# Renumbering the inner columns of a two-matrix expert layer: long rows of w_out, stepped weights from w_in

## The chip, the core and the metric

The kernel runs on one core of a Trainium2 chip. A core has a matrix engine (PE, TensorE, which loads weights and then streams columns past them), three engines for element work (DVE is VectorE, ACT is ScalarE, POOL is GpSimd), a queue engine for transfers (SP), and 16 DMA engines between the DRAM and the on-chip memory of 128 partitions. PE writes into accumulators (PSUM), from which ACT and DVE copy. The metric is the device time of one execution in microseconds; the median of several runs is compared.

## The reference

Attention with sketched features, followed by an expert layer with a rational activation:

```python
x = attention(q, k, v, S1, S2)          # 4352 tokens x 128
h = x @ w_in                            # w_in 128 x 2048
P = a[0] + a[1] * h + a[2] * h**2 + a[3] * h**3
Q = 1.0 + abs(b[0]) * abs(h) + abs(b[1]) * h**2
out = (P / (Q + 1e-6)) @ w_out          # w_out 2048 x 128
```

q, k and v are 4 batches x 4 heads x 1088 positions x 32, in float32. The 2048 inner columns of `h` are only ever used one by one and then summed over by `w_out`, so any numbering of them gives the same result as long as the columns of `w_in` and the rows of `w_out` are numbered alike.

## The kernel before

The attention part makes `xT`, a 128 x 4352 float32 tile with the model dimension on the partitions, batch by batch. The expert part runs over 17 units: one of the first 256 tokens, 14 for seven blocks of 512 tokens (each block in two units, one for each half of the inner columns), and two of 256 tokens at the end. A unit always has 4096 columns of work per partition, made of inner blocks of 128 columns by its tokens: 16 blocks by 256 tokens or 8 blocks by 512.

In a unit, `hidden` (line 448) multiplies: the weights are a 128 x 128 block of `w_in`, the moving operand is a stretch of `xT`; the result, 128 inner columns on the partitions by the tokens, goes to one of two `h_ps` accumulators. Everything there is float32, and one such product runs as two passes, each with its own weight load. There are 48 products of 256 columns and 112 of 512. ACT copies each accumulator to bf16 (`hh`, `evac`, line 454); DVE and ACT make |h|, the denominator, its reciprocal by logarithm and exponential, and the terms r, s and g (lines 477 to 562). `gather` (line 581) multiplies these with `w_out` as weights, in bf16, and adds all up in one accumulator for each block of tokens; `store` (line 590 on) transposes and writes the result.

The order of all instructions is written out by hand in `ORDER`, a list of steps such as `lw:1` (fetch half 1 of `w_out`), `lx:0` (fetch half 0 of `w_in`), `wo:3` (make a scaled bf16 copy of half of `w_out`), `h2:5` (line 448 for part 2 of unit 5) or `e2:5` (its copy). Each engine runs its own instructions in that order and waits only for the data and the buffers that it needs. Nothing is rescheduled at run time.

The fetches all go through SP's queue. After the first batch's k, q and v its order is: half 1 of `w_out`, the rest of q, half 0 of `w_out`, half 1 of `w_in`, the second batch's k, half 0 of `w_in`, the second batch's q and v. `w_out` is 1 MB in all, as is `w_in`; each half is 512 KB. `w_out_sb_f` has a partition for each of the 128 rows of an inner block, and along it 16 blocks of 128 float32. It is read six times (lines 614, 616 and 618), to make the three bf16 copies that `gather` uses: each half plain, times a[1] and times a[2].

Before the change, inner column number `128 * fo + fi` is row `fi` of block `fo`. So a partition of `w_out_sb_f` is filled from 16 separate rows of 512 bytes each, and the weights of a product are 128 neighbouring columns of `w_in_sb`.

Of the kernel before, what the change touches and what calls it, by code (L numbers as in the profile page):

```python
# [59 lines left out]
SPLIT_A = (0, 9, 13, 16)  # L60
QUARTER = (16,)
LX = 2
TAIL = 2
WIDE_S = (3, 5)
WIDE_M = (5,)
# [4 lines left out]
def kernel(  # L70
# [13 lines left out]
    nc = tc.nc  # L84
# [5 lines left out]
    nf = d_ff // 128  # L90
# [48 lines left out]
    for i, s_in in enumerate((S1, S2)):  # L139
        t = consts.tile([128, D], FP, name=f"s_raw{i}")  # L140
# [4 lines left out]
                      in_=bass.AP(tensor=k.tensor, offset=k.offset, ap=[[S * D // 32, 128], [W, NM], [1, 4 * D]]))  # L145
    nc.scalar.dma_start(out=k0[:, 0:km].rearrange("p (m x) -> p m x", m=NM - 1)[:, :, 4 * D:],
                        in_=k0_src[:, 0:km].rearrange("p (m x) -> p m x", m=NM - 1)[:, :, 4 * D:])
# [11 lines left out]
    load_v(0)  # L159
    w_in_sb = big.tile([d_model, d_ff], FP, name="w_in_sb")  # L160
    w_out_sb_f = mid.tile([128, nf, d_model], FP, name="w_out_sb_f", tag="w", bufs=2)
    w_out_src = moe_w_out.rearrange("(fo fi) d -> fi fo d", fi=128)

    idle = consts.tile([128, 512], BF, name="idle")
    nc.vector.memset(idle, 0.0)
# [27 lines left out]
    for i in range(2):  # L193
        t = consts.tile([128, D], FP, name=f"sT{i}")
# [14 lines left out]
    for i in range(2):  # L209
        t = consts.tile([128, 2, R, R], FP, name=f"SAB{i}")  # L210
# [14 lines left out]
    def wide():  # L225
        return hps.tile([128, 1024], FP, name="h_ps")
# [205 lines left out]
    t1 = n_tok % TC  # L432
    last = TC // TAIL
    for t0, tl in [(0, t1)] * (t1 > 0) + [(t, TC) for t in range(t1, n_tok - TC, TC)] + [(t, last) for t in range(n_tok - TC, n_tok, last)]:
# [7 lines left out]
    def hidden(i, part):  # L442
        t0, tl, f0, per = units[i]
        assert ready.issuperset(range(t0, t0 + tl, 64))
        t = live[i]["h", part] = wide()
        for x in range(per // 4):
            f = f0 + part * (per // 4) + x
            nc.tensor.matmul(t[:, x * tl:(x + 1) * tl], lhsT=w_in_sb[:, f * 128:(f + 1) * 128],  # L448
                             rhs=xT[:, t0:t0 + tl], start=True, stop=True)

    def evac(i, part):
# [188 lines left out]

    def fetch_w(x):
        f = slice(x * (nf // 2), (x + 1) * (nf // 2))
        nc.sync.dma_start(out=w_out_sb_f[:, f], in_=w_out_src[:, f])

    def fetch_x(x):
        c = slice(x * (d_ff // 2), (x + 1) * (d_ff // 2))
# [4 lines left out]
    blocks = [lambda: QA, lambda: QB, lambda: QC, once(lambda: Spread(0, q0, cuts[3], cuts[4]))]  # L651
    blocks += [once(lambda b=b, c0=c0, c1=c1: Spread(b, fetched["lq", b], c0, c1)) for b in range(1, B) for c0, c1 in spans]
    does = {"e": evac, "h": hidden, "u": d_abs, "w": d_w, "y": d_y, "ln": a_ln, "ex": a_exp, "pa": a_p, "pd": d_p,
            "s": d_s, "m": d_hs, "v": d_v, "x": d_g, "G": gather}
    q_does = {"qt": "transposes", "qs": "sketches", "qc": "copies", "qf": "features", "qp": "products", "qd": "plus",
# [55 lines left out]
```

## Time and profile before

| | |
|---|---|
| median of 3 runs | 274.04 us (273.96 to 274.20) |
| the profiled execution | 274.08 us, of which its span is 272.3 us |
| granted PE clock | 0.999 |
| DMA | 30530 packets, 19.55 MB, mean 72 GB/s |
| line 448, passes of 512 columns | 224, together 103.7 us busy |
| line 448, passes of 256 columns | 96, together 22.5 us busy |
| line 448, weight loads | 320, 58.3 us busy |
| line 581, products with w_out | 460, in bf16 |

The span is the time from the first to the last instruction that the profile holds; a run's time also has what lies around it. PEld is the weight loading of PE, told apart from its matmuls because the two overlap. A matmul's recorded length holds more than its streaming time, so the pace of a series is read from starts, not from lengths. A share of busy time is a mean over the span. The first 20 us are those with the most transfer: the DMA engines move 166, 290 and 330 GB/s in the first three of 40 slices of the span.

### The profile page before, as it was taken

The page shows a single profiled execution, that of the slowest core. Times are in us where ns is not written, and L with a number is a line of the kernel's source. Part 1 is how long each engine was busy: PE and PEld are TensorE (multiplying, and loading weights), DVE is VectorE, ACT ScalarE, POOL GpSimd, SP SyncE. Part 2 cuts the span into 40 slices and gives each one's busy share as a digit, 9 for nine tenths or more (in the row PEclk, how much of TensorE's full clock was granted, in tenths as well). Part 3 has the DMA queues.
Part 4 walks back from the last instruction along what each step waited for, and adds up shares of the span by engine and source line. Part 5 has one row for each costly group of instructions (what it writes and reads, how often), then busy time and mean ns, then how long its engine had stood idle before and what let it go on. Part 6 is the DMA issues. An engine that isn't in the chain of part 4 may idle for free.

```text
span 272.3 us, 3730 instructions
## 1 busy us (share of the span) xinstructions
PE 258.4 (95%) x1398; PEld 146.2 (54%) x1398; DVE 256.0 (94%) x277; ACT 250.2 (92%) x224; POOL 2.9 (1%) x24
## 2 busy tenths in 40 slices
PE   7989999999999899999999999999999998999763
PEld 2778656963564354545454554434545356675552
DVE  2876999999999999999999999999999999999993
ACT  1467999998999999999999999999999999999990
POOL 4000000000000000000000000000000000000000
PEclk9999999999999999999999999999999999999999
DMA  6993606314026052232304000120036100010004
GB/s 166 290 330 99 196 14 183 101 50 100 2 80 135 12 136 81 67 78 39 96 6 115 12 0 4 40 90 0 14 97 90 25 0 0 2 24 14 1 7 74
DMA packets 30530, 19.55 MB, mean 72 GB/s; under 512 B 20400, under 2 KB 26672, under 8 KB 30512
## 3 DMA queue, kind: packets, MB, share of 16 engines
q1 hardware_dynamic: 28992, 18.93, 27.2%
q10 hardware_dynamic: 1520, 0.38, 0.7%
q8 instruction: 11, 0.18, 0.3%
q14 instruction: 7, 0.06, 0.1%
HBM read 16.16 MB, written 3.15 MB: 71 GB/s over the span
## 4 chain that ended last, share of the span: by engine, by line
PE 35%; ACT 28%; DVE 23%; issue 9%; DMA 2%; SPq 1%; DVEq 0%; ACTq 0%
PE h_ps L448 17%; PE att_ps L581 9%; ACT hh L454 8%; ACT ln L539 7%; ACT r L543 7%; DVE s L547 4%; ACT p L534 4%; DVE g L551 4%; PE att_ps L361 3%; DVE g L562 3%; DVE w L488 3%; DVE w L483 2%; DMA k_sb<-in_k_dram 2%; PE att_ps L298 1%; PE att_ps L257 1%
## 5 line engine op out<-in xcount | busy, mean ns | idle before, releaser
L448 PE MATMUL h_ps<-xT,w_in_sb 128*128 128x512 f32 (+1 forms) x320 | 126.2, 536 | 2.3 <-ACT hh L454 1.6
L448 PEld LDWEIGHTS h_ps<-xT,w_in_sb 128*128 128x128 f32 x320 | 58.3, 190 | 52.8 <-issue 35.0
L454 ACT CAST hh<-h_ps 128x1024 bf16<-128x1024 f32 x68 | 68.2, 1022 | 4.2 <-PE h_ps L448 3.7
L581 PEld LDWEIGHTS <-w_out 128*128 128x128 bf16 x460 | 44.6, 98 | 46.0 <-issue 15.1
L543 ACT ACTIVATE r<-ln 128x2048 bf16<-128x2048 f32 (+1 forms) x35 | 65.9, 1883 | 0.3
L539 ACT ACTIVATE ln<-w 128x2048 f32<-128x2048 bf16 (+1 forms) x35 | 65.9, 1882 | 0.3
L534 ACT ACTIVATE p<-hh,a_sb 128x2048 bf16<-128x2048 bf16 (+1 forms) x23 | 46.7, 2035 | 0.1
L547 DVE TENSOR_TENSOR s<-hh,r 128x2048 bf16<-128x2048 bf16 (+2 forms) x33 | 40.9, 1243 | 0.2
L488 DVE TENSOR_TENSOR w<-w,u 128x4096 bf16<-128x4096 bf16 (+2 forms) x22 | 39.5, 1798 | 0.1
L581 PE MATMUL att_ps<-g,w_out 128*128 128x512 bf16 (+1 forms) x160 | 34.8, 347 | 3.6 <-DVE g L562 3.6
L551 DVE TENSOR_TENSOR g<-hh,s 128x2048 bf16<-128x2048 bf16 (+1 forms) x30 | 35.2, 1175 | 0.0
L581 PE MATMUL att_ps<-r,w_out 128*128 128x512 bf16 (+1 forms) x160 | 35.0, 347 | 0.0
L562 DVE TENSOR_TENSOR g<-g,p 128x2048 bf16<-128x2048 bf16 (+1 forms) x30 | 34.9, 1175 | 0.0
L581 PE MATMUL att_ps<-s,w_out 128*128 128x512 bf16 (+1 forms) x140 | 29.8, 343 | 0.9 <-DVE s L547 0.9
L483 DVE TENSOR_SCALAR w<-u,b_abs 128x4096 bf16<-128x4096 bf16 (+2 forms) x22 | 23.9, 1092 | 0.1
L477 DVE TENSOR_SCALAR u<-hh 128x4096 uint16<-128x4096 uint16 (+2 forms) x22 | 21.2, 968 | 0.9 <-ACT hh L454 0.8
L361 PEld LDWEIGHTS att_ps<-kvz,q_pT 128*128 128x128 f32 x144 | 17.6, 191 | 4.9 <-ACT sk_sb L408 1.0
L361 PE MATMUL att_ps<-kvz,q_pT 128*128 128x66 f32 x144 | 18.0, 274 | 0.9 <-DVE q_pT L353 0.5
L298 PEld LDWEIGHTS att_ps<-v_sb,k_p 128*64 128x64 f32 (+1 forms) x288 | 8.8, 138 | 2.6 <-issue 1.8
L529 DVE TENSOR_SCALAR p<-hh,a_sb 128x2048 bf16<-128x2048 bf16 x12 | 9.6, 799 | 0.0
L298 PE MATMUL att_ps<-v_sb,k_p 128*64 128x64 f32 (+1 forms) x288 | 9.5, 224 | 0.0
L425 DVE TENSOR_TENSOR q_pT<-a_all,b_all 128x768 f32<-128x768 f32 (+1 forms) x10 | 9.0, 896 | 0.0
(60 smaller groups left out, 135.1 us busy)
## 6 DMA issues: line engine op xcount, KB each, us to landing
a_all<-sk_d SPq DMA_DIRECT2D x6, 384.0 KB
b_all<-sk_d SPq DMA_DIRECT2D x12, 192.0 KB
v_sb<-in_v_dram SPq DMA_DIRECT2D x12, 144.0 KB
k_sb<-in_k_dram SPq DMA_DIRECT2D x3, 544.0 KB
q_sb<-in_q_dram SPq DMA_DIRECT2D x3, 544.0 KB
a_all<-sk_d SPq DMA_DIRECT2D x4, 320.0 KB
b_all<-sk_d SPq DMA_DIRECT2D x8, 160.0 KB
w_out_sb_f<-in_moe_w_out_dram SPq DMA_DIRECT2D x2, 512.0 KB
```

Source lines behind the costliest of these rows:

```text
L361: nc.tensor.matmul(self.nd[:, o:o + 2 * KW], lhsT=self.q_p[:, c, x:x + 128], rhs=kvz[self.b % 2][:, c, :], start=True, stop=True)
L448: nc.tensor.matmul(t[:, x * tl:(x + 1) * tl], lhsT=w_in_sb[:, f * 128:(f + 1) * 128], rhs=xT[:, t0:t0 + tl], start=True, stop=True)
L454: nc.scalar.copy(out=live[i]["hh"][:, part * PW:(part + 1) * PW], in_=live[i]["h", part])
L483: nc.vector.tensor_scalar(out=t[:, c], in0=live[i]["u"][:, c], scalar1=ab1, scalar2=ab0, op0=AX.mult, op1=AX.add)
L488: nc.vector.tensor_mul(out=t[:, c], in0=t[:, c], in1=live[i]["u"][:, c])
L534: nc.scalar.activation(out=part_of(i, "p", h), in_=hh, func=ACT.Identity, scale=a3, bias=a2)
L539: nc.scalar.activation(out=t, in_=live[i]["w"][:, span(h)], func=ACT.Ln, bias=1.0 + 1e-6)
L543: nc.scalar.activation(out=part_of(i, "r", h), in_=live[i]["ln"], func=ACT.Exp, scale=-1.0)
L547: nc.vector.tensor_mul(out=part_of(i, "s", h), in0=hh, in1=part_of(i, "r", h))
L551: nc.vector.tensor_mul(out=part_of(i, "g", h), in0=hh, in1=part_of(i, "p" if horner(i, first(h)) else "s", h))
L562: nc.vector.tensor_mul(out=g, in0=g, in1=part_of(i, "s" if horner(i, first(h)) else "p", h))
L581: nc.tensor.matmul(outs[t0][:, :tl], lhsT=w_sb[y][:, f0 + x, :], rhs=part_of(i, key, h)[:, c:c + tl], start=done[0] == 0, stop=done[0] == ...
```

## The change

The inner columns are numbered anew: column `1024 * a + 8 * fi + fo` is now row `fi` of block `8 * a + fo`, for the halves a = 0 and 1. A partition's eight rows of `w_out` in one half are then neighbours in DRAM, 4096 bytes in one piece. The tile `w_out_sb_f` and everything that reads it keep their shape. To match, the weights of a product in `hidden` are every eighth column of a half of `w_in_sb`: 128 float32 with a step of eight, where they were 128 neighbours. The transfer of `w_in` itself is as before. `PERM` is not read by anything. The order of the instructions on every engine, and their number, stay as they are.

```diff
@@ -159,7 +160,8 @@
     w_out_sb_f = mid.tile([128, nf, d_model], FP, name="w_out_sb_f", tag="w", bufs=2)
-    w_out_src = moe_w_out.rearrange("(fo fi) d -> fi fo d", fi=128)
+    w_out_src = moe_w_out.rearrange("(a fi fo) d -> a fi (fo d)", a=2, fi=128)
+    w_in_blocks = w_in_sb.rearrange("p (a fi fo) -> p a fo fi", a=2, fi=128)
@@ -445,7 +447,7 @@
             f = f0 + part * (per // 4) + x
-            nc.tensor.matmul(t[:, x * tl:(x + 1) * tl], lhsT=w_in_sb[:, f * 128:(f + 1) * 128],
+            nc.tensor.matmul(t[:, x * tl:(x + 1) * tl], lhsT=w_in_blocks[:, 2 * f // nf, f % (nf // 2)],
                              rhs=xT[:, t0:t0 + tl], start=True, stop=True)
@@ -640,7 +642,7 @@
         f = slice(x * (nf // 2), (x + 1) * (nf // 2))
-        nc.sync.dma_start(out=w_out_sb_f[:, f], in_=w_out_src[:, f])
+        nc.sync.dma_start(out=w_out_sb_f[:, f].rearrange("p f d -> p (f d)"), in_=w_out_src[x])
```

More of the change, by code (lines that the diff above doesn't have):

```diff
@@ L62 @@
 LX = 2
+PERM = 1
 TAIL = 2
```

## The prediction

> **What bounds the kernel now.** I read the busy table first, then the chain of waits in order of time, then the timeline of the first 31 us, then the groups by shape.
>
> ```profile
> span 272.3 us, 3730 instructions
> PE 258.4 (95%) x1398; PEld 146.2 (54%) x1398; DVE 256.0 (94%) x277; ACT 250.2 (92%) x224; POOL 2.9 (1%) x24
> L448 PE MATMUL h_ps<-xT,w_in_sb 128*128 128x512 f32 (+1 forms) x320 | 126.2, 536 | 2.3 <-ACT hh L454 1.6
> L448 PEld LDWEIGHTS h_ps<-xT,w_in_sb 128*128 128x128 f32 x320 | 58.3, 190 | 52.8 <-issue 35.0
> ```
>
> Three engines are within three points of each other, so none has slack to give away for long. The 160 float32 products of line 448 run as 320 passes, each with a weight load of its own (PEld, 190 ns). The change touches exactly these 320 loads and the two transfers of w_out. Which of the engines sets the pace where is in the chain:
>
> ```profile
> 19.06 3.51 PE h_ps L448 x16
> 22.57 0.84 PE att_ps L361 x8
> 23.41 3.51 PE h_ps L448 x16
> ...
> 42.58 3.49 PE h_ps L448 x8
> ...
> 93.26 3.70 PE h_ps L448 x8
> ...
> 178.70 1.98 PE h_ps L448 x4
> ```
>
> Columns: start, length, what. From 12.6 to 66 us the chain is PE almost without a break, and line 448 is its longest part; then it passes to ACT (66 to 118), DVE (124 to 170), PE again (178 to 200), ACT and at the end DVE. In all, 15 stretches of line 448 lie on it (17% of the span). Two paces come out of it: a pass of 256 columns takes 3.51/16 = 219 ns, one of 512 columns 3.49/8 = 436 ns.
>
> ```profile
> 11.50 1.15 ACT L616 ACTIVATE w_out<-w_out_sb_f,a_sb 128x1024 bf16<-128x1024 f32 x1
> 17.95 0.97 PEld L361 LDWEIGHTS att_ps<-kvz,q_pT 128*128 128x128 f32 x8 [0.76 <-DVE q_pT L353]
> 18.84 3.33 PEld L448 LDWEIGHTS h_ps<-xT,w_in_sb 128*128 128x128 f32 x16
> 22.09 1.04 DVE L321 STREAM_TRANSPOSE qT<-q_sb 128x384 f32<-128x384 f32 x2 [2.13 <-DMA q_sb<-in_q_dram]
> 23.65 0.69 DVE L477 TENSOR_SCALAR u<-hh 128x2048 uint16<-128x2048 uint16 x1 [0.23 <-ACT hh L454]
> ```
>
> The brackets give an engine's idle time and what ended it. Line 361 shows what a load costs when nothing but loads limits PE: eight take 0.97 us, so they start (0.97 - 0.19)/7 = 111 ns apart, though each is recorded as 190 ns long. So a load occupies its path for 111 ns, and behind a pass of 219 or 436 ns it costs nothing: it is done long before the pass in front of it ends.
>
> **The change, part by part.** *The w_out transfers.* Two DMAs of 512 KB, issued in the same places of SP's queue (0.43 us of issue each, as now). Each partition's 4 KB of a half now lies together in DRAM. In the trace's packet records the 2048 packets of w_out are 512 bytes long and a 512-byte packet takes 30 ns; w_in already comes in 4096-byte packets of 172 ns. On 16 DMA engines that is 2048 x 30/16 = 3.84 us before and 256 x 172/16 = 2.75 us after: 1.1 us of transfer time freed before 18 us. Nobody waits for it. The ACT and DVE lines that read w_out (616, 614, 618; the first at 11.50) have no bracket, so they start as soon as their engine is free. The one compute wait on a DMA behind it in the queue is DVE's 2.13 us for the next batch of q at 22.09; it would shrink to about 1.0. But DVE then reaches line 477 earlier and waits there for hh, which ACT finishes at 23.62 because PE delivers it then, and PE is what the chain runs through. I take 0 us; if that cover were gone it would be a gain of 1.1 us at most. [...]
>
> *The weights.* The number of loads stays 320, of 128 columns each, but the columns now stand eight float32 apart in the partition. No row of this trace has such a load, so I bound it. Lower end: it costs as much as now, 111 ns; a gain is excluded, because the columns are no fewer. Upper end: it sweeps all 1024 words between its first and last column. The 512-column pass gives 436/512 = 0.85 ns per float32 word, so 1024 words are 870 ns, 760 more than now. A row of a far engine points up too: line 372 on ACT reads float32 33 apart (from the partial sums), 155 ns for 8 elements and 211 ns on average for 12, which is 14 ns for each further element; but DVE's line 369 reads 8 of the same in 146 ns, less than the 200 ns of a contiguous line 376. The value I take is near the low end, since the closest row is the same load on the same engine: one doubling of the time per column. A load of 64 columns (line 298) is 138 ns, one of 128 is 190, so a column is 52/64 = 0.81 ns and doubling 128 of them adds 104 ns. The load then occupies 111 + 104 = 215 ns.
>
> Against 436 ns per 512-column pass (224 of them) that stays hidden. Against 219 ns per 256-column pass (96 of them, in the first block of tokens and the last two) it just fits; I allow nothing. What is not hidden is the first load of a group, when nothing long runs in front of it: after a wait for a free h_ps buffer, or after the short passes of lines 361, 257 and 402 (at most 111 ns apart). Of the 15 stretches of line 448 on the chain, those at 97.83, 184.14 and 188.44 follow line 581's 512-column passes (215 ns) and hide it; 12 are exposed: 12 x 0.104 = 1.25 us. In all of the trace 32 such loads can be found; if each were on the path it would be 32 x 0.104 = 3.3 us. What is late behind an exposed load: its pass, the hh copy (ACT, line 454) and with it u on DVE.
>
> Sum: 274.08 (the profiled run's own time: span 272.30 and 1.78 around it) + 0 + 1.25 = 275.3. The median of the runs shown is 274.04, so the two are the same for this purpose. **Forecast 275.3 us**, its own range 274.6 to 277.4 (half the chain's exposures, all 32).
>
> [...]
>
> **The rivals.**
> *No price.* The stepped load costs 111 ns as now. For it: a float32 column already takes 0.85 ns on PE, twice the 215/512 = 0.42 ns of a bf16 one, so there may be room for a slower read; against it, only line 372. Both edits are then free: 274.0, within 273.6 to 274.5.
> *A heavier load.* Three times the time per column: 111 + 208 = 319 ns. Now the 256-column passes wait for it, 319 - 219 = 100 ns each. The first block's 32 passes lie on the chain (19.06 and 23.41): 3.2 us. The last two blocks' 64 (224 to 248 us) would lose 6.4, where the chain is on ACT and DVE but PE is 97% busy too: half of it. With 12 x 0.208 = 2.5 exposed this gives 274.1 + 3.2 + 3.2 + 2.5 = 283; 280 to 287. From 219 ns of occupancy on, this case decides. Against it: no engine here reads float32 at a third of its usual rate for lack of contiguity, apart from the few elements of line 372.
> *Faster.* The freed 1.1 us reaches the end: q lands at 21.0 instead of 22.1, DVE's wait shrinks by as much, and all after it moves up: 273.0. It decides only if DVE sets the pace at 22 us and the loads cost nothing. For it: the 2.13 us wait is real, and DVE is 94% busy. Against it: DVE idles 0.23 us for ACT right after, and PE, not DVE, carries the chain from 12.6 to 66 us.
> *The change doesn't shorten the packets.* Since the transfers are counted at 0, the time is that of the forecast.
>
> **How the numbers follow.** Forecast 0.37, no price 0.29, heavier 0.22, faster 0.10, and 0.02 for a load dearer still. About 0.2% (0.55 us) is what a measurement of this kernel tells from no change. Slower by more: the forecast, the heavier cases, less the forecast's lowest edge: 0.60. Within: 0.30. Faster: 0.10. The range reaches down to no price (273.6) and up into the heavier case as far as its middle (283.5), leaving out the faster case and the top of the heavier one, about 0.2. As the forecast and no price have different signs of effect, the forecast's own 274.6 to 277.4 stands beside it.
>
> **What would show each step.** The weight loads of line 448: 190 ns recorded now, some 294 if a column takes twice as long, 398 if three times, 190 if free. The pace of the first 256-column group (3.67 us for 16 passes): unchanged in the forecast, about 5.3 us in the heavier case. The 512-column pass: 436 ns in all cases but the upper end. Start of line 477's first instruction: 23.65 in the case without price, 23.9 in the forecast (two exposed loads). DVE's wait at 22.09: about 1.0 us, if packets of w_out are 4096 bytes long (some 1800 packets fewer in the queue's count). The forecast is wrong if the loads stay at 190 ns, if passes of 512 columns get longer, or if the wait for q shrinks and the end moves with it.

## The result, and the profile after

The changed kernel takes 276.56 us (median of 5 runs, 276.49 to 276.66) against 274.04 us before in the same comparison: 1.0093 times as long, 95% interval 1.008 to 1.0107. That is 2.5 us more, where 1.25 us more were forecast.

The busy table and the two groups of line 448 (now line 450; the two added lines shift all that stand below them), from the page of the changed kernel:

```profile
span 274.8 us, 3714 instructions
PE 261.5 (95%) x1382; PEld 178.8 (65%) x1398; DVE 256.3 (93%) x277; ACT 250.6 (91%) x224; POOL 2.9 (1%) x24
DMA packets 28738, 19.55 MB, mean 71 GB/s; under 512 B 20400, under 2 KB 24624, under 8 KB 28720
L450 PE MATMUL h_ps<-xT,w_in_sb 128*128 128x512 f32 (+1 forms) x320 | 131.1, 553 | 1.8 <-ACT hh L456 1.4
L450 PEld LDWEIGHTS h_ps<-xT,w_in_sb 128*128 128x128 f32 x320 | 91.2, 322 | 28.2 <-ACT hh L456 6.5
```

DVE, ACT and POOL are as busy as before to within 0.4 us. What grew is PEld, by 32.6 us, and PE by 3.1 us (16 matmul records are missing from this trace, so a little more). A weight load of line 450 is recorded at 322 ns on average instead of 190. The packets fell by 1792, which is 2048 packets of 512 bytes less and 256 of 4096 bytes more: the transfers did what they were changed to do.

The chain of waits of the changed kernel, in order of time (start, length, what):

```profile
18.95 3.99 PE h_ps L450 x16
22.93 0.84 PE att_ps L363 x8
23.77 3.99 PE h_ps L450 x16
...
30.78 7.17 PE h_ps L450 x16
...
43.68 3.61 PE h_ps L450 x8
```

These stand beside the same pieces of the prediction. The two groups of sixteen 256-column passes went from 3.51 to 3.99 us, 0.48 us more each. A group of eight 512-column passes went from 3.49 to 3.61, 0.12 us more, once for the whole group. PE's share of the chain rose from 35% to 61%: with loads of 322 ns instead of 190 PE sets the pace in stretches where ACT (28% before, 24% now) or DVE (23%, now 6%) did.

And the timeline of the same time:

```profile
17.84 0.97 PEld L363 LDWEIGHTS att_ps<-kvz,q_pT 128*128 128x128 f32 x8 [0.76 <-DVE q_pT L355]
18.72 3.91 PEld L450 LDWEIGHTS h_ps<-xT,w_in_sb 128*128 128x128 f32 x16
18.78 4.15 PE L450 MATMUL h_ps<-xT,w_in_sb 128*128 128x256 f32 x16
20.90 1.04 DVE L323 STREAM_TRANSPOSE qT<-q_sb 128x384 f32<-128x384 f32 x2 [1.05 <-DMA q_sb<-in_q_dram]
24.02 0.69 DVE L479 TENSOR_SCALAR u<-hh 128x2048 uint16<-128x2048 uint16 x1 [1.79 <-ACT hh L456]
```

The contiguous loads of line 363 still take 0.97 us for eight. The sixteen stepped ones take 3.91 us where they took 3.33; by their start times the 256-column passes follow each other every 240 ns (median) instead of 216, and the load beside them has no idle time left. DVE gets its q 1.2 us earlier and gives all of it back at once: its wait for hh before line 479 is 1.79 us instead of 0.23.

Pairing ACT's 224 instructions of both traces in order, the changed kernel is 0.12 us ahead at 18 us, 0.85 behind at 27, 1.47 at 68, 1.76 at 178, 2.16 at 241 and 2.66 at 255. (Times are those of the kernel before.) So 1.0 us is lost in the first unit of 256 tokens, then 1.3 us in small pieces over 14 units of 512 tokens, and 0.5 us in the last two units of 256.

### The profile page after: what moved, and what is told of

It is laid out like the page before. It is cut to its first block, busy times and chain, and to the rows that moved or that the text cites. A ratio compares the mean times of both kernels' runs of the same rounds, so it can differ in the third digit from the quotient of the medians.

```text
span 274.8 us, 3714 instructions
## 1 busy us (share of the span) xinstructions
PE 261.5 (95%) x1382; PEld 178.8 (65%) x1398; DVE 256.3 (93%) x277; ACT 250.6 (91%) x224; POOL 2.9 (1%) x24
## 4 chain that ended last, share of the span: by engine, by line
PE 61%; ACT 24%; DVE 6%; issue 5%; DMA 2%; SPq 1%; DVEq 0%; ACTq 0%
PE h_ps L450 33%; PE att_ps L583 16%; ACT ln L541 7%; ACT r L545 6%; ACT hh L456 6%; PE att_ps L363 4%; ACT p L536 3%; PE att_ps L300 2%; PE att_ps L259 2%; DMA k_sb<-in_k_dram 2%; DVE s L549 2%; DVE g L553 1%; PE att_ps L404 1%; PE att_ps L389 1%; DVE g L564 1%
## 5 line engine op out<-in xcount | busy, mean ns | idle before, releaser
L450 PE MATMUL h_ps<-xT,w_in_sb 128*128 128x512 f32 (+1 forms) x320 | 131.1, 553 | 1.8 <-ACT hh L456 1.4
L450 PEld LDWEIGHTS h_ps<-xT,w_in_sb 128*128 128x128 f32 x320 | 91.2, 322 | 28.2 <-ACT hh L456 6.5
L583 PE MATMUL att_ps<-g,w_out 128*128 128x512 bf16 (+1 forms) x153 | 33.8, 346 | 3.3 <-DVE g L564 2.9
L583 PE MATMUL att_ps<-r,w_out 128*128 128x512 bf16 (+1 forms) x154 | 33.8, 346 | 0.4 <-issue 0.2
L485 DVE TENSOR_SCALAR w<-u,b_abs 128x4096 bf16<-128x4096 bf16 (+2 forms) x22 | 23.9, 1092 | 0.1
```

Of the source, the lines that this page charges most:

```text
L450: nc.tensor.matmul(t[:, x * tl:(x + 1) * tl], lhsT=w_in_blocks[:, 2 * f // nf, f % (nf // 2)], rhs=xT[:, t0:t0 + tl], start=True, stop=True)
L485: nc.vector.tensor_scalar(out=t[:, c], in0=live[i]["u"][:, c], scalar1=ab1, scalar2=ab0, op0=AX.mult, op1=AX.add)
L583: nc.tensor.matmul(outs[t0][:, :tl], lhsT=w_sb[y][:, f0 + x, :], rhs=part_of(i, key, h)[:, c:c + tl], start=done[0] == 0, stop=done[0] == ...
```

## The experiments

All were timed against the kernel before on the same chip. Three labels recur: the *weights* edit is the `lhsT=` line of the diff, the *rows* edit is the pair of `w_out` lines.

**The two halves of the change, one at a time.**

```diff
-            nc.tensor.matmul(..., lhsT=w_in_blocks[:, 2 * f // nf, f % (nf // 2)],
+            nc.tensor.matmul(..., lhsT=w_in_sb[:, f * 128:(f + 1) * 128],
```

This, made to the changed kernel (dots stand for code left out here), leaves the rows edit alone.

> w_out in rows of 4096 bytes, the weights of line 448 contiguous as before; the rows of w_out then do not match the columns of w_in, so only the time counts. Theory A (all of the loss is the stepped weight loads, the transfers are free): 274.0 us, within 0.3 of before, although DVE's wait for q at 22 us falls from 2.1 to about 1.1 us. Rival B (earlier transfers bring a gain that the loads then eat): 273.0 us, and the loads alone would cost about 3.5 us. Rival C (the transfers cost something themselves): over 274.5 us.

Measured: 274.02 us, ratio 1.0005 (0.9992 to 1.0018). The timeline of DVE:

```profile
20.40 1.04 DVE L323 STREAM_TRANSPOSE qT<-q_sb 128x384 f32<-128x384 f32 x2 [0.73 <-DMA q_sb<-in_q_dram]
21.37 0.37 DVE L253 STREAM_TRANSPOSE kT<-k_sb 128x224 f32<-128x224 f32 x1
23.36 0.69 DVE L479 TENSOR_SCALAR u<-hh 128x2048 uint16<-128x2048 uint16 x1 [1.62 <-ACT hh L456]
```

The wait for q falls from 2.13 to 0.73 us, and the wait for hh behind it grows from 0.23 to 1.62 by the same 1.4 us. (This execution as a whole began 0.3 us earlier, with the first k.) Nothing is passed on. Rivals B and C fall.

The opposite, the weights edit alone on the kernel before:

> Weights with a step of eight in all 320 loads, w_out loaded in rows of 512 bytes as before (numbers do not match, only the time counts). Theory A: 276.5 us, the same as the whole change. Rival B: 277.5 us. Rival C: under 276.1 us.

Measured: 276.69 us, ratio 1.0095 (1.0082 to 1.0108), with loads of 322 ns as in the whole change. All of the loss is the stepped loads.

**Which of the loads.** The weights edit, in the units of one size only:

```diff
+            nc.tensor.matmul(..., lhsT=w_in_blocks[:, 2 * f // nf, f % (nf // 2)] if tl == 256 else w_in_sb[:, f * 128:(f + 1) * 128],
```

> Weights with a step of eight only in the three units of 256 tokens (96 passes of 256 columns); only the time counts. Theory A1 (a stepped load occupies 240 ns, so the passes of 256 columns are stretched from 214 to 240 ns, and exposed first loads cost some 0.12 us each): first unit 32 x 0.026 + 2 x 0.12 = 1.1 us, of the last two units' 64 x 0.026 = 1.7 us about half: 275.5 to 276.0 us, with passes at 240 ns. Rival A2 (as forecast: the passes of 256 columns hide the load, only first loads cost): 274.3 us.

Measured: 275.56 us, ratio 1.0049 (1.0036 to 1.0063): 1.5 us for 96 of the 320 loads.

> Weights with a step of eight only in the 14 units of 512 tokens (224 passes of 512 columns); only the time counts. Theory A1: the passes stay at 429 ns, ten or so exposed first loads on the path at 0.12 us: 275.0 to 275.3 us. Rival A2 (all of the loss lies in exposed first loads): 276.2 us.

Measured: 275.47 us, ratio 1.0054 (1.0039 to 1.0068): 1.4 us for the other 224. That is 0.2 us above theory A1's figure, which the interval (275.1 to 275.9 us) takes in; rival A2's 276.2 it does not. The groups by shape, first of the 256-column kernel, then of the 512-column one:

```profile
L449 PE MATMUL h_ps<-xT,w_in_sb 128*128 128x512 f32 x224 | 103.7, 602 | 1.6 <-ACT hh L455 0.9 <-ACT xT L392 0.2
L449 PE MATMUL h_ps<-xT,w_in_sb 128*128 128x256 f32 x96 | 24.8, 408 | 0.4 <-ACT hh L455 0.4
```

```profile
L449 PE MATMUL h_ps<-xT,w_in_sb 128*128 128x512 f32 x224 | 106.3, 615 | 1.3 <-ACT hh L455 1.0 <-ACT xT L392 0.4
L449 PE MATMUL h_ps<-xT,w_in_sb 128*128 128x256 f32 x96 | 22.5, 382 | 0.7 <-ACT hh L455 0.7
```

Busy time of the 256-column passes is 22.5 us with contiguous weights and 24.8 with stepped ones, 2.3 us or 24 ns for each of 96; 1.5 us of it reaches the end. The 512-column passes go from 103.7 to 106.3, but their pace by starts stays at 429 ns. So in the one kind every pass is longer, and in the other a few are much longer. Rival A2, the forecast's own view of the 256-column passes, falls. (By the median of starts a 256-column pass takes 216 ns with contiguous weights, not the 214 of the expectations.) Paired with the kernel before as above, ACT loses 0.97 and 0.49 us in the first and the last two units of the 256-column kernel and 0.06 between, and 1.32 us over the 14 units of the 512-column one. In the whole change it goes from 0.12 us ahead to 2.66 behind, 2.78 us in all, which is the sum of the three losses.

**Only the head of a group, or all but the head.** In a unit of 512 tokens a group is two products. The step for the first product only (`x == 0`), and for the second only (`x > 0`):

> Weights with a step of eight only for the first of the two products in each of the 56 groups of 512 columns; only the time counts. Theory A1 (in these units only the load at the head of a group costs, because nothing long runs in front of it): the same as with the step in all of their products, 275.3 to 275.5 us. Rival H (every stepped load costs a little, by the more that it reads beside the running pass): half of that, 274.7 us.

> The complement: step of eight only for the second product of each group of 512 columns, whose loads run behind a pass of 429 ns; only the time counts. Theory A1: 274.0 us, the same as before, though 112 loads are recorded at 315 ns. Rival H: 274.7 us.

Measured: 275.10 us, ratio 1.004 (1.0026 to 1.0054), and 273.81 us, ratio 1.0 (0.9986 to 1.0015).

```profile
L449 PEld LDWEIGHTS h_ps<-xT,w_in_sb 128*128 128x128 f32 x320 | 72.1, 233 | 42.6 <-issue 18.5 <-ACT hh L455 9.2 <-ACT xT L392 2.4
L449 PE MATMUL h_ps<-xT,w_in_sb 128*128 128x512 f32 x224 | 103.7, 602 | 1.5 <-ACT hh L455 0.9 <-ACT xT L392 0.2
```

These two lines are of the kernel with the step behind the first. Its loads are busy for 72.1 us instead of 58.3, and its 512-column passes for 103.7, exactly as before the change. Paired with the kernel before, its ACT loses nothing between 18 and 255 us, to 0.01 us. A stepped load behind a pass of 429 ns is free here (273.81 us against 273.99 before); at the head of a group, with nothing long in front of it, it costs its whole extra length, 315 ns against 190 (the first passes of the forecast's twelve heads are recorded 121 to 126 ns longer in the changed kernel). The kernel with the step at the heads alone loses 1.25 us of ACT's time between 27 and 255 us, nearly the 1.32 us of the kernel with all 224. The first-of-group kernel is 0.2 us below theory A1's figure; its interval reaches up to 275.5 (1.0054 x 273.99) and excludes neither that figure nor, at its lower end, rival H's 274.7. It is the other kernel that rules H out.

**What the step costs by its size.** The same renumbering with 2, 4 and 16 neighbouring rows instead of 8, and a step of three on overlapping stretches of `w_in`:

```diff
+    w_out_src = moe_w_out.rearrange("(a fi fo) d -> fi a (fo d)", fi=128, fo=STEP)
+    w_in_blocks = w_in_sb.rearrange("p (a fi fo) -> p a fo fi", fi=128, fo=STEP)
...
+            nc.tensor.matmul(..., lhsT=w_in_blocks[:, f // STEP, f % STEP],
...
```

The transfers of `w_out` are cut up to match. For the step of three only the weights change: `lhsT=w_in_sb[:, f * 108:f * 108 + 382:3]`.

> The same renumbering with two rows instead of eight: w_out in pieces of 1024 bytes, weights of line 448 with a step of two float32 (8 bytes). Theory L (a load pays for each 16-byte stretch that it touches without a second hit in it): loads recorded at 190 ns as before, 256-column passes at 214 ns, 274.0 us. Rival S (the price grows with the span that is swept): some 10 to 30 ns more per load than the 111 ns of contiguous ones, 274.2 to 274.5 us. Rival U (any step other than one costs the full price): 240 ns per pass, 276.6 us.

> The same with four rows: pieces of 2048 bytes, a step of four float32 (16 bytes), so that every column starts a new 16 bytes. Theory L: the full price as with a step of eight, passes of 256 columns at 240 ns, 276.6 us. Rival S: between, 275.0 us, loads shorter than with a step of eight. Rival U: 276.6 us.

> The same with sixteen rows: pieces of 4096 bytes out of 8192, a step of sixteen float32 (64 bytes). Theory L and rival U: no dearer than a step of eight, passes at 240 ns, 276.6 us. Rival S: twice the extra of a step of eight, 370 ns per load, passes of 256 columns at about 370 ns, over 285 us.

> Weights of line 448 with a step of three float32 (12 bytes), taken from overlapping stretches of w_in, w_out as before: numbers do not match, only the time counts. Four columns lie in three stretches of 16 bytes. Theory L: one of two to three columns gets a second hit, a price between none and full; as the 256-column pass hides 214 ns, 274.3 to 275.8 us. Rival U: 276.6 us.

The load groups of the kernels with a step of 2, 3, 4 and 16, one line from each:

```profile
L450 PEld LDWEIGHTS h_ps<-xT,w_in_sb 128*128 128x128 f32 x320 | 60.3, 196 | 51.1 <-issue 34.1 <-ACT hh L456 11.3 <-ACT xT L393 2.3
```

```profile
L448 PEld LDWEIGHTS h_ps<-xT,w_in_sb 128*128 128x128 f32 x320 | 75.7, 255 | 41.6 <-issue 26.1 <-ACT hh L454 9.6 <-ACT xT L391 2.3
```

```profile
L450 PEld LDWEIGHTS h_ps<-xT,w_in_sb 128*128 128x128 f32 x320 | 89.5, 316 | 29.2 <-ACT hh L456 6.6 <-ACT xT L393 2.1 <-issue 0.8
```

```profile
L450 PEld LDWEIGHTS h_ps<-xT,w_in_sb 128*128 128x128 f32 x320 | 85.4, 300 | 32.9 <-ACT hh L456 7.3 <-ACT xT L393 2.2 <-ACT sk_sb L410 1.0
```

| step (bytes) | load, median ns | pace of 256-column passes, median ns | time, us | ratio, 95% interval |
|---|---|---|---|---|
| 1 (4) | 190 | 216 | 274.04 | |
| 2 (8) | 196 | 216 | 274.18 | 1.0 (0.9991 to 1.0008) |
| 3 (12) | 252 | 216 | 276.28 | 1.0069 (1.0047 to 1.0092) |
| 4 (16) | 309 | 233 | 276.29 | 1.0081 (1.0068 to 1.0093) |
| 8 (32) | 315 | 240 | 276.56 | 1.0093 (1.008 to 1.0107) |
| 16 (64) | 298 | 222 | 275.88 | 1.0069 (1.0051 to 1.0087) |

The kernel before took 274.15 us in the comparison of steps 2, 3, 4 and 16. For step 3 the time is the median of five executions, 275.26 to 277.78 us; a sixth took 279.86.

The price, the load's median less 190 ns, is there nearly in full from 16 bytes on (119, 125 and 108 ns), half of it at 12 bytes (62 ns), and next to nothing at 8 bytes (6 ns). At 12 bytes, of four neighbouring columns two share a stretch of 16 bytes and two are alone in theirs: half of the columns, and half of the price. The price does not grow with the span swept (125 ns with a step of eight, 108 with sixteen), so S falls, and it is not the same for any step (6 ns with two, 125 with eight), so U falls. The load lengths fit theory L at each step tried. A trace shows how long a load takes, not what it reads, so what goes on within a load is not shown.

The times of steps 3 and 16 are not to be compared with the rest: the first product of line 448, a block of the upper half, there reads from both halves of `w_in` instead of one, and both profiles show PE waiting about 1.0 us before it. This is the line of the matmuls with a step of 16:

```profile
20.42 1.89 PE L450 MATMUL h_ps<-xT,w_in_sb 128*128 128x256 f32 x7 [0.93 <-ACT sk_sb L410]
```

The bracket names ACT's `sk_sb`, but that copy had ended at 19.65 us. By the trace's semaphore records the last piece of half 0 of `w_in` lands at 20.33 us, 0.09 before this line starts; with step 3 it lands at 20.02 us and PE starts at 20.11.

The profiled execution of step 3 (277.78 us) lost more behind that wait: its granted clock was 0.50 from 20.16 to 23.57 us, and the passes there followed each other every 427 ns. Its mean clock is 0.994. The two other executions with that mean took 277.17 and 279.86 us, the three with a higher one 275.26 to 276.28. So step 3's load length answers the question of L and U, its time does not.

No kernel of these is faster than the one before: the step of two has `w_out` in pieces of 1024 bytes instead of 512 at no price (274.18 us, ratio 1.0), and gains nothing, as the rows edit with its pieces of 4096 bytes gained nothing (1.0005).

## Why the prediction was right or wrong

*The w_out transfers at 0 us*: right. The packets are as counted, DVE's wait for q shrinks to 1.05 us (1.0 was forecast), and the cover named, DVE's wait for hh, takes it up at once. The rows edit alone gives 1.0005. The rival "faster" is out for the reason given against it. The longer packets did move more, but by less than the forecast took from the mean times of w_in's packets: 4096 bytes take 205 ns on average in the changed kernel, 25.6 for each 512 bytes, against 30 for a packet of 512 before and 21.5 by the 172 ns of the forecast. Here that was worth nothing.

*A price for the stepped load, one doubling of the column's time*: right, and right in size at the head of a group, where no stepped load runs in front. Forecast were 104 ns more and an occupancy of 215 ns. At the first head of the changed kernel the second load starts 216 ns after the first (112 before the change), and the first is recorded 120 ns longer than before:

```profile
18.72 0.31 PEld L450 LDWEIGHTS h_ps<-xT,w_in_sb 128*128 128x128 f32 x1
18.94 0.34 PEld L450 LDWEIGHTS h_ps<-xT,w_in_sb 128*128 128x128 f32 x1
```

In a series behind 256-column passes it is dearer: the loads are recorded at 337 ns and follow each other every 240.

*"Against 219 ns per 256-column pass it just fits; I allow nothing"*: this is the step that failed. It put the 96 passes of 256 columns at nothing, and they cost some 1.2 of the 2.8 us by which ACT falls behind: 0.7 in the first unit (0.97 less two heads) and 0.5 in the last two. 215 against 219 left no margin for an estimate put together from lengths of other loads. The pace of 219 was itself read too long, from a piece of the chain that ends with the recorded end of a matmul (379 ns is the median length of these passes before the change); by starts it is 216. And the occupancy of a load by itself was taken for that of a load in a series, where a load starts 7 ns after the pass in front of it (median of the first group) and its own pass 233 ns after that, 240 in all. So each pass is longer by 24 ns. Why a load in a series takes longer than the 216 ns was not tried. The kernel with the step only in these units loses 1.5 us, where the forecast had 0.21 for them (two heads of groups on the chain). The rival "heavier load" had this mechanism, deciding from 219 ns on, with 100 ns per pass; the truth lies between the two, nearer the forecast. Of the 64 passes at the end that rival took half as reaching the end; of 64 x 24 = 1.5 us some 0.5 do.

*Twelve exposed heads of groups at 104 ns*: right in mechanism and nearly in price (121 to 126 ns), but the count came out partly by luck. Ten of them belong to 512-column passes, 1.04 us; the kernel with the step there alone loses 1.4, the one with the step at the heads 1.1, the complement nothing. Paired with the kernel before, ten such heads do reach ACT, 1.3 us in all, but not the same ten. The heads at 93.26 and 100.83 us, on the chain before, cost ACT nothing: it stays 1.48 us behind from 92 to 112 us. Two at about 142 and 208 us, where the chain ran through DVE and ACT, cost 0.12 and 0.13. The chain of the kernel before is not wholly that of the changed one.

*The sum* was 1.25 us for a loss of 2.5. The two parts measured alone are 1.5 and 1.4, within their intervals the 2.65 of the weights edit as a whole. The direction and the range held; the passes put at nothing are what it lacked.

*The signs to look for*: loads of 294 ns were named for a doubling and 398 for a tripling; 312 to 338 are seen. The 512-column pace was to stay, and does (429 ns by starts; the 436 was read like the 219). The first group's 3.67 us were to stay in the forecast, and are 4.15. Line 477's start was to be 23.9 in the forecast; it is 24.02.

*The size of the step*: the forecast had one price for a stepped load, one doubling, with the sweep of all words, 760 ns more, as its upper end. In the runs the price depends on the step: 8 bytes cost 6 ns per load of 128 columns, 12 bytes 62 ns, 16 bytes and more 108 to 125 ns, about one nanosecond for a column. Nothing ahead of these runs showed the 16 bytes of theory L; the lengths of the loads fit them. That a step of 64 bytes (298 ns) is a little cheaper than one of 32 (315 ns) the theory does not tell.

## What to carry to other kernels

A transfer made shorter is worth what its last waiter gives up, and a wait that another one follows directly gives up nothing (with the rows edit alone the wait for q fell by 1.4 us, the wait for hh behind it grew by 1.4, and the time ratio was 1.0005); look for that second wait before counting. Here a stepped load of 315 ns was hidden by a pass of 429 ns in front of it (273.81 us against 273.99), and in a series behind 256-column passes (337 ns a load) it stretched them from 216 ns to 240; so price a slower load by the shortest pass and by the heads of groups, not by the mean; and when two estimates differ by 2% at such an edge, put the other side of the edge into the forecast. Heads counted on the chain before the change give the size of the loss, not the places: a change that slows one engine moves the chain (PE's share of it went from 35% to 61%). A step of two float32, 8 bytes, was almost free for float32 weights here (6 ns per load, time ratio 1.0): if rows are to lie together, two of them did it at no price.

## What the runs showed of the hardware

A step of sixteen is a little cheaper than one of eight: loads of 298 against 315 ns, and 222 against 240 ns for the pace of 256-column passes. Why was not tried. With a step of eight, the loads that start less than 250 ns after another stepped load are recorded at 334 to 338 ns, 121 of 122, and the others at 312 to 322: the 256-column passes have nearly all of the first kind, the 512-column passes only the second load of an exposed head. Why was not tried either. In the profiled execution of step 3 the granted clock was 0.50 for 3.41 us behind a wait of PE of 0.98 us; behind waits of 0.93 us (step 16) and 0.92 us (the kernel before, at 93 us) it stayed at 1.00. What decides between the two no run here shows.
